# Attention into a gated convolution on one core: batch 0's x in rows of 4 KB, one maximum per batch on the read path, a new order of emission

## The chip, the cores and the metric

The kernel runs on one core of a Trainium2 chip. The metric is the device time of one execution in microseconds (us). The time before is 356.75 us, the median of 3 runs (355.89 to 357.86).

## The reference

Eight batches of attention in both directions between a sequence `x` (8 heads, 512 tokens, 64 wide) and a state of 32 tokens per head; the two results, put behind each other, are the 544 tokens of a gated feed-forward layer with a convolution over three tokens.

```
scores = scale * np.matmul(x, state.transpose(0, 1, 3, 2))
a = np.exp(scores - scores.max(-1, keepdims=True))
a /= a.sum(-1, keepdims=True) + 1e-09
xread = np.matmul(a, state)
scores2 = scale * np.matmul(state, x.transpose(0, 1, 3, 2))
a2 = np.exp(scores2 - scores2.max(-1, keepdims=True))
a2 /= a2.sum(-1, keepdims=True) + 1e-09
sread = np.matmul(a2, x)
t = np.concatenate([xread, sread], axis=2)         # heads side by side: 8 x 544 x 512
h = np.maximum(t @ w_in, 0.0)                       # 8 x 544 x 1024
conv_out[:, s] = sum of conv_w[k] * h[:, s + k - 1] for k in 0, 1, 2
out = (h / (1 + np.exp(-conv_out))) @ w_out         # 8 x 544 x 512
```

## The kernel before, in words

**Work.** The 1024 hidden columns are cut into 8 blocks of 128. A step is one block of one batch, 64 steps in all, named by a number `i` from 0 to 63 (batch `i // 8`, block `i % 8`): the hidden product into a bank `ps_h_i` (`hidden`, L630, six products of 512 columns), its rectified copy `h_i` (L200 on ScalarE, L202 on VectorE), the three taps into `t_i` (L194 or L196, then L673 and L678), the tanh (L682), the gate (L687), the split of the gated tile into two halves of fewer bits, `g0_i` (L205, ScalarE) and `g1_i` (L208, VectorE), and for each of four chunks `c` of 128 tokens three products into the bank `acc_b_c` (L705). A float32 product is made of three products of such halves (`PASSES`). After a batch's eighth block the chunks are copied out of their banks (L719 on ScalarE, L721 on VectorE) and stored (L740).

**The state's own tokens** go four batches at a time (`m` is 0 or 1), block by block, through the same layer: `ss_m_f` (L745, L749 twice, L752, L756), then `gts0_m_f` and `gts1_m_f` (L205, L208), then three products into `acc_t_m` (L705) and a store of four parts (L775). There is one buffer `ss`, so a block's chain begins when the last one's has ended.

**The read path** of a batch (what a state token reads of `x`): the scores' copy `at` is 128 rows by two head groups of 512; per group a maximum (`top`, L340), an exponential with its sum (`exp2`, L346), the reciprocal of that sum (`norm2`, L349 and L350), a transposition (`flip`, L355) and its copy, then `read` (L368) and a copy with the reciprocal as scale (`divide`, L375).

**Batch 0** has a path of its own, since nothing stands ahead of it. Its `x` comes as two tiles, each with all four pairs of heads and one half of the sequence, and everything is done by halves `q` of the sequence: `first_scores` (L320), the scaled copy of the scores (`keep_scores`, L194 or L196), `first_flip` (L488), the maximum (`first_top`, L492), the subtraction of it by TensorE (`first_shift`, L498), the exponential (L508), the sums (L512), their reciprocal (L516, L517), its spreading (L498), the division (L523), and the first hidden products (`first_hidden`, L637). The columns of the weights that batch 0 needs come as 64-bit words in tiles `raw_j` and are converted by ScalarE and VectorE on the way (L243 to L260), between the pieces of batch 0.

**Order.** Every operation of the program is entered in a list with what it reads and writes. Nothing schedules them: the table `ORDER`, written by hand, is a row of numbers of operations, and the program is emitted in that order; each engine does its part of it in that order. A `v` behind a number puts the operation on VectorE in place of ScalarE, and a negative number is so many products of zeros (L215) that keep TensorE occupied. SP issues the loads and all the stores but the last two, which ScalarE's own queue issues (`LAST`).

Of the kernel before, what the change touches and what calls it, by code (L numbers as in the profile page):

```python
# [953 lines left out]
```

## Time and profile before

| what | value |
|---|---|
| median of 3 runs | 356.75 us (355.89 to 357.86) |
| profiled execution | span 354.1 us; no other time of it is listed, and what lies around the span is taken as 356.75 - 354.1 = 2.65 us |
| TensorE (PE) busy | 98% of the span, 2538 products |
| VectorE (DVE) busy | 89% |
| ScalarE (ACT) busy | 72% |
| DMA | 35.06 MB, mean 99 GB/s |

The profile is one execution's trace. Its first line counts each engine's busy time; its chain of waits goes back from the last instruction to what released each; the groups of instructions give a mean time for one line, engine and shape; the timeline tells runs of like instructions in order with what ended the idle time before them; the windows give each engine's busy time, the granted clock and what the DMA engines moved in a stretch. The clock that TensorE was granted was 1.00 of full speed (2.4 GHz) in every stretch.

### The profile page before, as it was taken

Reading aid. Unit: us, or ns where it says so; the run is one execution under the profiler, and the core shown is the slowest. Engines: PE = TensorE matmul, PEld = TensorE weight load, DVE = VectorE, ACT = ScalarE, POOL = GpSimd, SP = SyncE. Lnnn points to the kernel's source line nnn. Section 1 sums busy time; section 2 is a strip of 40 time slices with the busy share of each in tenths; the row PEclk is TensorE's granted clock in tenths of the full one; section 3 lists DMA queues with packets and bytes.
Section 4 is the critical chain, followed back from the end, with each engine's and each line's share of the span. In section 5 each row is a group of like instructions: output and inputs, shape, how many; then the busy total and the mean of one; then the engine's idle time right before and its main releaser. Section 6 shows DMA issues by size and latency. Waiting matters only on the chain.

```text
span 354.1 us, 6694 instructions
## 1 busy us (share of the span) xinstructions
PE 348.6 (98%) x2538; PEld 271.8 (77%) x2538; DVE 316.1 (89%) x563; ACT 256.1 (72%) x560; POOL 29.4 (8%) x90
## 2 busy tenths in 40 slices
PE   7999999999999999999999999999999999999995
PEld 6766758876788868878789887878788868888884
DVE  1999999999999999999999999987799898889950
ACT  3999999998777997859856657774745447548642
POOL 1000000010000000100000300042201001113000
PEclk9999999999999999999999999999999999999999
DMA  7989998201600033030400000001200011000205
GB/s 255 396 309 377 328 357 302 62 1 50 219 0 2 0 127 142 3 119 32 180 30 2 0 31 31 30 3 60 89 2 0 0 71 65 2 2 0 74 33 176
DMA packets 13584, 35.06 MB, mean 99 GB/s; under 512 B 1520, under 2 KB 4720, under 8 KB 12528
## 3 DMA queue, kind: packets, MB, share of 16 engines
q1 hardware_dynamic: 12976, 34.28, 27.1%
q8 instruction: 20, 0.33, 0.4%
q10 hardware_dynamic: 576, 0.35, 0.3%
q14 instruction: 12, 0.10, 0.1%
HBM read 25.71 MB, written 8.91 MB: 98 GB/s over the span
## 4 chain that ended last, share of the span: by engine, by line
PE 97%; DMA 2%; ACT 0%; SPq 0%; issue 0%
PE acc L705 47%; PE ps_h L630 22%; PE ps_h L637 4%; PE ps_hs L615 4%; PE ps_u L548 4%; PE acc_t L705 3%; PE ps_r L368 2%; PE ps_t L355 2%; PE ps_s L310 2%; DMA xt<-xT 2%; PE acc_c L705 2%; PE acc L713 2%; PE ps_u L567 1%; PE ps_s L498 1%; PE ps_x L498 1%; PE ps_x L512 1%
## 5 line engine op out<-in xcount | busy, mean ns | idle before, releaser
L705 PE MATMUL acc<-wo,g 128*128 128x512 f32 x726 | 177.0, 393 | 0.0
L705 PEld LDWEIGHTS acc<-wo,g 128*128 128x128 f32 x726 | 134.7, 188 | 32.8 <-issue 1.7
L630 PE MATMUL ps_h<-a,u 128*128 128x512 f32 x336 | 83.2, 391 | 0.0
L630 PEld LDWEIGHTS ps_h<-a,u 128*128 128x128 f32 x336 | 62.7, 188 | 13.1
L682 ACT ACTIVATE t<-t 128x512 f32<-128x512 f32 x64 | 39.9, 630 | 14.5 <-DVE t L678 14.3
L673 DVE SCALAR_TENSOR_TENSOR t<-h,cw,t 128x511 f32<-128x511 f32 x64 | 47.1, 742 | 1.6 <-ACT t L194 1.5
L678 DVE SCALAR_TENSOR_TENSOR t<-h,cw,t 128x512 f32<-128x512 f32 (+1 forms) x64 | 46.8, 745 | 0.6
L205 ACT ACTIVATE g<-t 128x512 fp32r<-128x512 f32 (+1 forms) x62 | 37.5, 615 | 11.0 <-DVE t L687 5.5
L687 DVE SCALAR_TENSOR_TENSOR t<-t,h 128x512 f32<-128x512 f32 (+1 forms) x64 | 42.4, 667 | 2.3 <-ACT t L682 2.2
L208 DVE TENSOR_TENSOR g<-t,g 128x512 fp32r<-128x512 f32 (+1 forms) x62 | 41.3, 671 | 3.5 <-ACT g L205 3.1
L194 ACT ACTIVATE t<-h,cw 128x512 f32<-128x512 f32 x52 | 36.9, 723 | 4.3 <-DVE h L202 3.0
L200 ACT ACTIVATE h<-ps_h 128x512 f32<-128x512 f32 x56 | 33.3, 596 | 9.3 <-PE ps_h L630 6.1
L648 POOL COPY h<-hs 128x1 f32<-128x1 f32 x40 | 14.2, 376 | 129.2 <-ACT sr L383 66.3
L205 ACT ACTIVATE u<-ps_u 128x512 fp32r<-128x512 f32 x28 | 16.2, 596 | 8.5 <-PE ps_u L548 8.5
L719 ACT ACTIVATE o<-acc 128x512 f32<-128x512 f32 (+1 forms) x30 | 15.8, 544 | 8.5 <-PE acc L705 8.3
L648 POOL COPY hs<-h 128x1 f32<-128x1 f32 x40 | 13.6, 361 | 97.6 <-ACT h L200 80.9
L208 DVE TENSOR_TENSOR u<-ps_u,u 128x512 fp32r<-128x512 f32 x28 | 18.6, 682 | 2.5 <-ACT u L205 2.5
L615 PEld LDWEIGHTS ps_hs<-sr,wi 128*128 128x128 f32 x128 | 14.8, 192 | 1.1 <-ACT t L194 0.8
L637 PE MATMUL ps_h<-p,u 128*128 128x256 f32 x64 | 15.3, 386 | 0.0
L615 PE MATMUL ps_hs<-sr,wi 128*128 128x128 f32 x128 | 15.0, 276 | 0.0
L548 PE MATMUL ps_u<-wi,st 64*32 64x512 f32 x224 | 14.3, 597 | 0.0
L637 PEld LDWEIGHTS ps_h<-p,u 128*128 128x128 f32 x64 | 11.6, 190 | 3.3 <-DVE hc L249 0.8
(99 smaller groups left out, 400.3 us busy)
## 6 DMA issues: line engine op xcount, KB each, us to landing
xt<-xT SPq DMA_DIRECT2D x16, 512.0 KB, 7.7
xx<-xn SPq DMA_DIRECT2D x8, 1024.0 KB, 5.9
out<-o SPq DMA_DIRECT2D x27, 256.0 KB, 2.1
raw<-w_in SPq DMA_DIRECT2D x8, 512.0 KB, 7.6
raw<-w_out SPq DMA_DIRECT2D x8, 512.0 KB, 7.4
out<-o SPq DMA_DIRECT2D x6, 128.0 KB, 1.8
out<-o_t SPq DMA_DIRECT2D x8, 64.0 KB, 1.7
st<-stT SPq DMA_DIRECT2D x1, 448.0 KB, 10.2
```

What stands on the lines that cost most here:

```text
L194: A.activation(dst, src, AF.Copy, scale=scale)
L200: A.activation(dst, src, AF.Relu, scale=0.5)
L205: A.activation(hi, src, AF.Copy)
L208: engine.tensor_tensor(lo, src, hi.bitcast(F32), op=ALU.subtract)
L615: PE.matmul(ps_hs[m, f][:, :NT], wi[:, k, f * P:(f + 1) * P], sr[m][:, k, :], start=(k == 0), stop=(k == NK - 1))
L630: PE.matmul(ps_h[i], u[j][:, g, fs], a[k][:, g, :], start=(n == 0), stop=(n == 3 * NG - 1))
L637: PE.matmul(ps_h[f][:, q * HS:(q + 1) * HS], us[0, f // 4][0][:, g, f % 4 * P:(f % 4 + 1) * P], half_of(pa[0], q)[:, g, :], start=(g == 0) ...
L673: V.scalar_tensor_tensor(t[:, 1:], h[:, :S - 1], cw[:, f, 0:1], t[:, 1:], op0=ALU.mult, op1=ALU.add)
L678: V.scalar_tensor_tensor(t[:, :n], h[:, 1:n + 1], cw[:, f, 2:3], t[:, :n], op0=ALU.mult, op1=ALU.add)
L682: A.activation(tt[i], tt[i], AF.Tanh, scale=0.25)
L687: V.scalar_tensor_tensor(tt[i][:, :n], tt[i][:, :n], 1.0, hd[i][:, :n], op0=ALU.add, op1=ALU.mult)
L705: PE.matmul(acc, g[j][:, cs], wo[:, k, f, :], start=(f == 0 and n == 0), stop=(f == NF - 1 and n == 2))
```

## The change

Three things change. Batch 0's two tiles of `x` hold two pairs of heads and the whole sequence each (a row of 4 KB for each of 128 partitions, in place of four rows of 1 KB), as all other batches' do; each half of the first scores then reads both tiles. The read path's maximum is taken for both head groups of a batch by one operation over 128 x 1024, and the sum and its reciprocal are one operation each for both groups, so that both exponentials wait for the one maximum and the reciprocal for both exponentials. The table of the order is written anew: it has 35 operations on VectorE by `v` in place of 25, and the same 16 products of zeros (12 of them ahead of the first scores in place of 9).

```
     def xt_load(i):
         b, g = divmod(i, NG)
-        if b == 0:
-            xts[i] = buf([P, NP, HS], F32, "xt", f"xt_{i}")
-            nc.sync.dma_start(xts[i], xT[b, :, :, g * HS:(g + 1) * HS])
-            return
         xts[i] = buf([P, 2, S], F32, "xt", f"xt_{i}")
         nc.sync.dma_start(xts[i], xT[b, :, 2 * g:2 * g + 2, :])
...
-                PE.matmul(ps_s[q][g][j * NS:(j + 1) * NS, :HS], st[half, j, :], xts[q][half, j, :],
+                PE.matmul(ps_s[q][g][j * NS:(j + 1) * NS, :HS], st[half, j, :], half_of(xts[j // 2], q)[half, j % 2, :],
...
-    def top(i):
-
-        b, g = divmod(i, NG)
-        nm2[i] = buf([P, 1], F32, "nm2", f"nm2_{i}")
-        V.tensor_reduce(nm2[i], at[b][:, g, :], axis=AX.X, op=ALU.max, negate=True)
+    def top(b):
+        nm2[b] = buf([P, NG], F32, "nm2", f"nm2_{b}")
+        s2[b] = buf([P, NG], F32, "s2", f"s2_{b}")
+        V.tensor_reduce(nm2[b], at[b], axis=AX.X, op=ALU.max, negate=True)
...
-        s2[i] = buf([P, 1], F32, "s2", f"s2_{i}")
-        A.activation(e2[i], at[b][:, g, :], AF.Exp, bias=nm2.pop(i), accum_out=s2[i])
-
-    def norm2(i):
-        V.tensor_scalar_add(s2[i], s2[i], EPS)
-        V.reciprocal(s2[i], s2[i])
+        A.activation(e2[i], at[b][:, g, :], AF.Exp, bias=nm2[b][:, g:g + 1], accum_out=s2[b][:, g:g + 1])
+
+    def norm2(b):
+        V.tensor_scalar_add(s2[b], s2[b], EPS)
+        V.reciprocal(s2[b], s2[b])
...
-            add("PE", "scoresh", partial(first_scores, q), r=[("st", 0), ("xt", q)],
+            add("PE", "scoresh", partial(first_scores, q), r=[("st", 0)] + [("xt", g) for g in range(NG)],
...
-        A.activation(rr[b][:, g, :], ps_r[b][:, g * D:(g + 1) * D], AF.Copy, scale=s2.pop(i))
+        A.activation(rr[b][:, g, :], ps_r[b][:, g * D:(g + 1) * D], AF.Copy, scale=s2[b][:, g:g + 1])
...
-0 98 99 100 101 102 103 120 -9 123 121 125 -3 124 -1 142 143 126 2 -2 150 3 127 5 20 4 144 151 128 6 -1 152 132 145
+120 -3 0 -8 98 99 -1 101 100 102 103 121 123 124 2 126v 125 127 -1 140 141 4 148 149 3 5 142 14 15 17 150 128 16 129
```

Lines of the changed kernel lie four to six below those of the one before: the first scores stand in L316 (L320 before), the maximum in L335 (L340), the sum in L343 and L344 (L349, L350), the last copies in L715 and L717 (L719, L721).

**VectorE at the start of the program.** `hc` and `raw` are the weights under conversion, `heads` a small constant, `m0_q` the maxima of half `q` of batch 0, `nm2` the maximum of the read path, `ps_s_0_1_g` the second half's scores of head group `g`. A wait on a DMAHW semaphore is one for a landing. Before:

```order
L182 TENSOR_REDUCE heads_75<-ident_69 128x4 [waits Pool_49]
L492 TENSOR_REDUCE m0_0_146<-ps_x_0_141 128x16 [waits PE_49]
L340 TENSOR_REDUCE nm2_0_161<-at_0_112 128x1 [waits Activation_49]
L249 TENSOR_SCALAR hc_0_159<-hc_0_159 128x512 [waits Activation_49]
L492 TENSOR_REDUCE m0_1_183<-ps_x_1_154 128x16 [waits PE_49]
L252 ISA hc_0_159<-raw_0_150,hc_0_159 128x1024 [waits DMAHW4_49,DVE_49,Activation_49]
L340 TENSOR_REDUCE nm2_1_206<-at_0_112 128x1
L260 SCALAR_TENSOR_TENSOR wi_79<-raw_0_150,hc_0_159 128x4x128 [waits DVE_49]
```

With the change:

```order
L196 TENSOR_SCALAR at_0_117<-ps_s_0_1_0_128 128x256 [waits PE_49]
L196 TENSOR_SCALAR at_0_117<-ps_s_0_1_1_129 128x256 [waits PE_49]
L182 TENSOR_REDUCE heads_75<-ident_69 128x4 [waits Pool_49]
L335 TENSOR_REDUCE nm2_0_144<-at_0_117 128x2 [waits DVE_49,Activation_49]
L488 TENSOR_REDUCE m0_0_153<-ps_x_0_148 128x16 [waits PE_49]
L488 TENSOR_REDUCE m0_1_161<-ps_x_1_156 128x16 [waits PE_49]
L249 TENSOR_SCALAR hc_0_163<-hc_0_163 128x512 [waits Activation_49]
L249 TENSOR_SCALAR hc_2_184<-hc_2_184 128x512 [waits Activation_49]
L252 ISA hc_0_163<-raw_0_138,hc_0_163 128x1024 [waits DMAHW4_49,DVE_49]
L252 ISA hc_2_184<-raw_2_182,hc_2_184 128x1024 [waits DMAHW5_49,DVE_49,Activation_49]
L260 SCALAR_TENSOR_TENSOR wi_79<-raw_0_138,hc_0_163 128x4x128 [waits DVE_49]
L260 SCALAR_TENSOR_TENSOR wi_79<-raw_2_182,hc_2_184 128x2x256 [waits DVE_49]
```

The copies of the second half's scores come onto VectorE, and the one wide maximum stands ahead of both of the halves' maxima; before, a maximum of the read path stood behind each of them.

**TensorE at the start.** `idle` are products of zeros, `ps_x_q` the transposed scores. Of the eight first scores of each half those that wait are shown, and of other groups the first. Before:

```order
L215 MATMUL idle_102<-zeros_67 128x128 x8
L320 MATMUL ps_s_0_0_0_113<-xt_0_100,st_81 32x256 [waits DMAHW1_49,DMAHW0_49]
...
L215 MATMUL idle_102<-zeros_67 128x128 x3
L320 MATMUL ps_s_0_1_0_130<-xt_1_123,st_81 32x256 [waits DMAHW3_49]
...
L215 MATMUL idle_102<-zeros_67 128x128
L488 MATMUL ps_x_0_141<-ident_69,at_0_112 128x128 [waits Activation_49,Pool_49]
...
L215 MATMUL idle_102<-zeros_67 128x128 x2
L488 MATMUL ps_x_1_154<-ident_69,at_0_112 128x128 [waits Activation_49]
...
L498 MATMUL ps_s_0_0_0_113<-eight_74,m0_0_146 32x128 [waits DVE_49,Pool_49]
...
L215 MATMUL idle_102<-zeros_67 128x128
L498 MATMUL ps_s_0_1_0_130<-eight_74,m0_1_183 32x128 [waits DVE_49]
```

With the change:

```order
L215 MATMUL idle_93<-zeros_67 128x128 x11
L316 MATMUL ps_s_0_0_0_118<-xt_0_91,st_81 32x256 [waits DMAHW1_49,DMAHW0_49]
...
L316 MATMUL ps_s_0_0_0_118<-xt_1_115,st_81 32x256 [waits DMAHW3_49]
...
L316 MATMUL ps_s_0_1_0_128<-xt_0_91,st_81 32x256
...
L215 MATMUL idle_93<-zeros_67 128x128
L484 MATMUL ps_x_0_148<-ident_69,at_0_117 128x128 [waits Activation_49,Pool_49]
...
L484 MATMUL ps_x_1_156<-ident_69,at_0_117 128x128 [waits DVE_49]
...
L494 MATMUL ps_s_0_0_0_118<-eight_74,m0_0_153 32x128 [waits DVE_49,Pool_49]
...
L494 MATMUL ps_s_0_1_0_128<-eight_74,m0_1_161 32x128 [waits DVE_49]
```

The first half's scores wait for both landings and not for one; the second half's follow at once, and the transpositions and shifts of the two halves stand together.

**The end of the program.** On TensorE, each row shown is followed by one with `g0` (or `gts0`) in place of `g1` (or `gts1`), two products, which is left out without a mark. Before:

```order
L705 MATMUL acc_t_1_3619<-wo_80,gts1_1_7_3928 128x512
L705 MATMUL acc_7_1_3789<-wo_80,g1_61_3889 128x512
L705 MATMUL acc_7_2_3761<-wo_80,g1_62_3908 128x512
L705 MATMUL acc_7_3_3737<-wo_80,g1_62_3908 128x512
L705 MATMUL acc_7_0_3741<-wo_80,g1_61_3889 128x512
L705 MATMUL acc_7_1_3789<-wo_80,g1_62_3908 128x512
L705 MATMUL acc_7_1_3789<-wo_80,g1_63_3935 128x512
L705 MATMUL acc_7_3_3737<-wo_80,g1_63_3935 128x512
L705 MATMUL acc_7_2_3761<-wo_80,g1_63_3935 128x512
L705 MATMUL acc_7_0_3741<-wo_80,g1_62_3908 128x512
L705 MATMUL acc_7_0_3741<-wo_80,g1_63_3935 128x512
```

With the change:

```order
L701 MATMUL acc_7_1_3736<-wo_80,g1_62_3829 128x512
L701 MATMUL acc_7_1_3736<-wo_80,g1_63_3864 128x512
L701 MATMUL acc_7_3_3756<-wo_80,g1_63_3864 128x512
L701 MATMUL acc_7_2_3681<-wo_80,g1_62_3829 128x512
L701 MATMUL acc_7_2_3681<-wo_80,g1_63_3864 128x512
L701 MATMUL acc_7_0_3695<-wo_80,g1_60_3790 128x512
L701 MATMUL acc_t_1_3573<-wo_80,gts1_1_6_3880 128x512
L701 MATMUL acc_t_1_3573<-wo_80,gts1_1_7_3929 128x512
L701 MATMUL acc_7_0_3695<-wo_80,g1_61_3807 128x512
L701 MATMUL acc_7_0_3695<-wo_80,g1_62_3829 128x512
L701 MATMUL acc_7_0_3695<-wo_80,g1_63_3864 128x512
```

The first use of `g1_63` moves from 15 products ahead of the end to 30, that of the last block of the state's tokens (`gts1_1_7`) from 33 to 12, and that of the block ahead of it (`gts1_1_6`, in an earlier row before) from 51 to 15. The last hidden product of step 63, ahead of these rows, moves from 165 products before the end to 105. On VectorE, the same stretch before:

```order
L749 SCALAR_TENSOR_TENSOR ss_1_7_3879<-hs_83,cw_78,ss_1_7_3879 128x128 [waits Activation_49]
L208 TENSOR_TENSOR g1_61_3889<-t_61_3662,g0_61_3888 128x512 [waits Activation_49]
L749 SCALAR_TENSOR_TENSOR ss_1_7_3879<-hs_83,cw_78,ss_1_7_3879 128x128 [waits DVE_49]
L687 SCALAR_TENSOR_TENSOR t_63_3724<-t_63_3724,h_63_3708 128x512
L687 SCALAR_TENSOR_TENSOR t_62_3753<-t_62_3753,h_62_3652 128x512
L721 TENSOR_SCALAR o_6_2_0_3910<-acc_6_2_3417 128x512 [waits DMAHW4_49,DMAHW7_49,DMAHW3_49,DMAHW0_49]
L756 SCALAR_TENSOR_TENSOR ss_1_7_3879<-ss_1_7_3879,hs_83 128x128 [waits Activation_49]
L208 TENSOR_TENSOR g1_62_3908<-t_62_3753,g0_62_3907 128x512 [waits Activation_49]
L208 TENSOR_TENSOR gts1_1_7_3928<-ss_1_7_3879,gts0_1_7_3927 128x128 [waits Activation_49]
L208 TENSOR_TENSOR g1_63_3935<-t_63_3724,g0_63_3934 128x512 [waits Activation_49]
L721 TENSOR_SCALAR o_7_1_0_3972<-acc_7_1_3789 128x256 [waits Activation_49]
```

With the change:

```order
L674 SCALAR_TENSOR_TENSOR t_63_3754<-h_63_3725,cw_78,t_63_3754 128x512
L683 SCALAR_TENSOR_TENSOR t_63_3754<-t_63_3754,h_63_3725 128x512 [waits Activation_49]
L208 TENSOR_TENSOR g1_63_3864<-t_63_3754,g0_63_3863 128x512 [waits Activation_49]
L745 SCALAR_TENSOR_TENSOR ss_1_6_3873<-hs_83,cw_78,ss_1_6_3873 128x128 [waits Activation_49]
L745 SCALAR_TENSOR_TENSOR ss_1_6_3873<-hs_83,cw_78,ss_1_6_3873 128x128 [waits DVE_49]
L752 SCALAR_TENSOR_TENSOR ss_1_6_3873<-ss_1_6_3873,hs_83 128x128 [waits Activation_49]
L208 TENSOR_TENSOR gts1_1_6_3880<-ss_1_6_3873,gts0_1_6_3879 128x128 [waits Activation_49]
...
L745 SCALAR_TENSOR_TENSOR ss_1_7_3900<-hs_83,cw_78,ss_1_7_3900 128x128 [waits Activation_49]
L745 SCALAR_TENSOR_TENSOR ss_1_7_3900<-hs_83,cw_78,ss_1_7_3900 128x128 [waits DVE_49]
L752 SCALAR_TENSOR_TENSOR ss_1_7_3900<-ss_1_7_3900,hs_83 128x128 [waits Activation_49]
...
L208 TENSOR_TENSOR gts1_1_7_3929<-ss_1_7_3900,gts0_1_7_3928 128x128 [waits Activation_49]
```

The chain of step 63 (`t_63`, `g1_63`) comes ahead of the last two blocks of the state's tokens, which now stand one behind the other at the very end.

## Rows read from the trace of the kernel before

**Rows 1.** The page: busy time, and the chain that ended last, by engine
```profile
PE 348.6 (98%) x2538; PEld 271.8 (77%) x2538; DVE 316.1 (89%) x563; ACT 256.1 (72%) x560; POOL 29.4 (8%) x90
...
PE 97%; DMA 2%; ACT 0%; SPq 0%; issue 0%
```

**Rows 2.** Groups by form: busy us, mean ns | idle before, for products of L705
```profile
L705 PE MATMUL acc<-wo,g 128*128 128x512 f32 x726 | 177.0, 393 | 0.0
```

**Rows 3.** Timeline of PE at 299 us: start, us, line, count
```profile
299.12 3.79 PE L705 MATMUL acc<-wo,g 128*128 128x512 f32 x16
```

**Rows 4.** Timeline of the first 20 us: start, us, engine, line, [idle, releaser]
```profile
0.71 1.31 SPq L295 DMA_DIRECT2D xt<-xT  x2
...
5.07 0.67 PE L320 MATMUL ps_s<-xt,st 64*32 64x256 f32 x16 [0.33 <-DMA xt<-xT]
...
6.53 0.43 SPq L894 DMA_DIRECT2D st<-stT  x1
...
7.17 0.67 PE L320 MATMUL ps_s<-xt,st 64*32 64x256 f32 x16 [0.57 <-DMA xt<-xT]
...
8.73 0.69 DVE L492 TENSOR_REDUCE m<-ps_x 128x16 f32<-128x512 f32 x1 [2.85 <-PE ps_x L488]
...
9.57 1.08 PE L498 MATMUL ps_s<-eight,m 128*32 128x128 f32 x32
...
11.00 1.08 PE L498 MATMUL ps_s<-eight,m 128*32 128x128 f32 x32
...
18.07 1.99 PE L637 MATMUL ps_h<-p,u 128*128 128x256 f32 x8
```

**Rows 5.** Windows at the start: PE, PEld, DVE, ACT, POOL, clock, DMA share, GB/s
```profile
4.00:6.00 2.00, 1.67 (x25) 1.09 (x25) 0.74 (x4) 0.53 (x3) 0.00 (x0) 1.00 1.03 323
...
6.00:8.00 2.00, 1.43 (x24) 0.83 (x23) 0.00 (x0) 0.55 (x3) 0.00 (x0) 1.00 1.06 381
...
14.00:16.00 2.00, 2.00 (x42) 1.80 (x39) 2.00 (x4) 2.00 (x6) 0.00 (x0) 1.00 1.02 406
```

**Rows 6.** Groups by form of the VectorE operations removed, added and moved
```profile
L340 DVE TENSOR_REDUCE nm<-at 128x1 f32<-128x512 f32 x16 | 10.8, 679 | 0.0
...
L437 DVE TENSOR_REDUCE m<-af 128x32 f32<-128x1024 f32 x7 | 8.5, 1215 | 0.1
...
L350 DVE RECIPROCAL s<-s 128x1 f32<-128x1 f32 x16 | 2.6, 164 | 0.5
...
L349 DVE TENSOR_SCALAR s<-s 128x1 f32<-128x1 f32 x16 | 2.3, 144 | 0.0
...
L721 DVE TENSOR_SCALAR o<-acc 128x256 f32<-128x256 f32 x1 | 0.4, 424 | 6.2 <-ACT o L719 6.2
```

**Rows 7.** Windows behind the start, columns as in rows 5
```profile
18.07:28.85 10.78, 10.78 (x148) 7.35 (x144) 10.72 (x22) 10.51 (x23) 0.00 (x0) 1.00 0.92 327
28.85:49.72 20.87, 20.83 (x254) 13.52 (x248) 20.35 (x44) 20.20 (x51) 0.00 (x0) 1.00 0.96 349
```

**Rows 8.** Timeline of the end
```profile
338.36 1.29 DVE L687 SCALAR_TENSOR_TENSOR t<-t,h 128x512 f32<-128x512 f32 x2
...
341.40 0.69 DVE L208 TENSOR_TENSOR g<-t,g 128x512 fp32r<-128x512 f32 x1 [0.15 <-ACT g L205]
...
343.57 6.96 PE L705 MATMUL acc<-wo,g 128*128 128x512 f32 x30
...
350.57 0.66 ACT L719 ACTIVATE o<-acc 128x256 f32<-128x256 f32 x2 [0.70 <-PE acc L705]
```

**Rows 9.** Groups by form of the chains of step 63 and of the state's tokens
```profile
L682 ACT ACTIVATE t<-t 128x512 f32<-128x512 f32 x64 | 39.9, 630 | 14.5 <-DVE t L678 14.3
...
L687 DVE SCALAR_TENSOR_TENSOR t<-t,h 128x512 f32<-128x512 f32 x56 | 37.9, 683 | 2.3 <-ACT t L682 2.2
...
L749 DVE SCALAR_TENSOR_TENSOR ss<-hs,cw,ss 128x128 f32<-128x128 f32 x32 | 11.0, 345 | 1.1 <-ACT ss L745 0.9
...
L752 ACT ACTIVATE ss<-ss 128x128 f32<-128x128 f32 x16 | 4.9, 304 | 7.4 <-DVE ss L749 7.2
```

More of the change, by code (lines that the diff above doesn't have):

```diff
@@ L119 @@
[L119 to L120 removed]
+120 -3 0 -8 98 99 -1 101 100 102 103 121 123 124 2 126v 125 127 -1 140 141 4 148 149 3 5 142 14 15 17 150 128 16 129
+-1 6 143 131 151 20 8 18 144 7 21 9 22 19 23 11 145 -1 24 10 26 27 133 134 12 152 153 25 13 50 196 445 446 146 147 154
+52 447 155 51 451 132 29 28 448 450 30 32 33 34 35 473 53 54 449 452 36 -1 31 37 453 1 185 186 188 195 198 199 200 201
@@ new lines @@
+1032 1033 1046 397 398 1009 992 1007 1060 1022 1024 1034 352 1057 1058 1023 1035 1038 353 1047 1074 354 1507 399 400
+1088 1039 1519 1006 1021 1515 1036 1037 355 1520 1521 1522 1523 356 361 1108 1089 1090 1075 1524 1061 1525 1526 1153
+1062 1109 1110 1048 1049 1063 1064 1050 1154v 1156 1155 1138 1054 1065 1076 1077 1139 974 975 1142v 1078 1141 1140
+1052 1067 1527 1079 1528 1529 1143 1144 1530 1145 1087 1091 1053 1532 1051 1066 1073 1080 1533 1123 1124 1092 1093 394
+362 365 1534 1146 1535 1536 1068 1083 973 366 1094 363 1081 1069 1084 1095 364 1112v 1113 395 1531 1096 1100 1101 1147
@@ new lines @@
+1082 1127v 1128 1183 1184 1198 1098 1187 1185 1186 1126 1114 1115 1168 1116 1117 1104 1125 1129 1130 1236 1118 1122
+1199 1131 1188 1105 1200 1132 1133 1111 1537 1538 1169 1172v 1099 1540 1157v 1119 1158 1159 1106 1107 1148 1170 1541
+1097 1542 1202v 1203 1102v 1204 1213 1160 1171 1137 1134 1543 1205 1149 1214v 1215 1161 1201 1544 1173 1174 1545 1546
+1237v 1239 1103 1120 1135 1150 1152 1121 1136 1251 1162 1266 1163 1164 1175 1176 1189 1151 1166 1217 1548 1252 401
+1218 1190 1191 1206 1165 433 1177 1178 1181 1240 1180 1192 1193 1539 1167 1182 1267 1269 1219 1220 1221 1238 1241 1222
@@ new lines @@
+1223 1207 1208 1281 1196 1211 1549 1226 1195 1550 1551 1179 1194 1209 402 403 1282v 404 1255 1256 1283 405 1242 1243
+1244 1270 1271 1224 1253 1257 1552 1197 1212 1258 1268 1272 1285v 1286 1228 1273 1259 1326 1274 1229 1327 1553 1227
+1341 1330v 1328 1342 1343 1554 1216 1331 1556 1557 1558 1559 1210 1225 1230v 1231 1275 1276 1245 1234v 1296 1246 1311
+1312 1287 1254 1344 1315v 1313 435 436 438 1329 437 1260 1261 1560 1297 1300v 440 1250 1332 1547 1555 443 1248 1298
+1263 1265 1278 1247 439 1299 1288 1289 434 1316 1317 1561 1562 441 1284 444 1301 1302 442 1314 1379 1569 1570 1380
@@ new lines @@
+1381 1235 1345 1563 1564 1232v 1382 1303 1566 1567 1233 1304 1262 1249 1277 1364 1264 1279 1439 1394 1318 1319 1346
+1347 1290 1280 1291 1293 1365 1367 1366 1305 1306 1333 1320 1308 1321 1571 1323 1334 1368 1369 1348 1440 1442 1443v
+1294 1309 1572 1573 1383 1574 1575 1565 1384 1444 1385 1292 1307 1585 1386 1387 1295 1310 1324 1335 1336 1395v 1576
+1339 1325 1349 1454 1586 1397 1587 1588 1441 1445 1589 1590 1591 1338 1446 1447 1350 1340 1409 1351 1568 1322 1337
+1577 1578 1396 1579 1580 1353 1352 1398 1399 1424 1354 1455 1410 1411 1370 1371 1388 1372 1389 1581 1400 1582 1583
@@ L121 @@
+1373 1360 1361 1425 1457 1374 1377 1413v 1593 1594 1414 1401 1458 1415 1375 1402 1403 1392 1355 1412 1459 1595 1596
+1597 1584 1416 1469 1470v 1598 1417 1356 1357 1599 1404 1376 1391 1418 1419 1592 1456 1472 1609 1473v 1378 1393 1390
[3 rows of a table added]
+1498v 1499 1625 1626 1467 1496 1627 1628 1629 1497 1489 1482 1494 1495 1490v 1491 1435 1624 1630 1631 1632 1450 1492v
+1633 1635 1637 1636 1465 1493 1480 1486 1484 1634 1485 1487
 """
@@ L388, in attention @@
             i = NG * b + g
-            add("SP", "load_xt" if b else "load_xth", partial(xt_load, i), w=[("xt", i)])
+            add("SP", "load_xt", partial(xt_load, i), w=[("xt", i)])
         add("SP", "load_x2", partial(x_load, b), w=[("xx", b)])
@@ L400, in attention @@
                 w=[("scores", b, g)] + [("at", b)] * (b > 0 and g == 0))
+        rows_of = [("at", b)] + [("scores", b, q) for q in range(NG)]
+        add("DVE", "wide", partial(top, b), r=rows_of, w=[("nm2b", b), ("s2b", b)])
         for g in range(NG):
             i = NG * b + g
-            rows_of = [("at", b)] + [("scores", b, q) for q in ([g] if b else range(NG))]
-            add("DVE", "red", partial(top, i), r=rows_of, w=[("nm2", i)])
-            add("ACT", "exp2", partial(exp2, i), r=rows_of + [("nm2", i)], w=[("e2", i), ("s2", i)])
-            add("DVE", "norm2", partial(norm2, i), w=[("s2", i)])
+            add("ACT", "exp2", partial(exp2, i), r=rows_of + [("nm2b", b), ("s2b", b)], w=[("e2", i), ("s2", i)])
+        add("DVE", "norm2", partial(norm2, b), r=[("s2", NG * b + g) for g in range(NG)], w=[("s2b", b)])
+        for g in range(NG):
+            i = NG * b + g
             add("PE", "flip", partial(flip, i), r=[("e2", i)], w=[("ps", "t", i)])
@@ L411, in attention @@
         for g, i in enumerate(pair):
-            add("ACT", "rr", partial(divide, i), r=[("ps", "r", b), ("s2", i)] + [("rr", b)] * g,
+            add("ACT", "rr", partial(divide, i), r=[("ps", "r", b), ("s2b", b)] + [("rr", b)] * g,
                 w=[("rq", b, g)] if g else [("rq", b, g), ("rr", b)])
```

32 lines of the change are left out of this document (10 added, 22 removed), and 64 rows, old and new, of the table ORDER.

## The prediction

> **What bounds the kernel now.** I read the page's busy line and chain first: TensorE is busy 348.6 of 354.1 us and the chain that ended last lies on it for 97% [rows 1]. So an operation of VectorE or ScalarE counts only where TensorE waits for it. Next, how full TensorE's own time is: the mean of a 512-column product is 393 ns [rows 2], but products overlap, and sixteen in a row take 3.79 us, of which the last is one whole mean, so the pitch is (3.79 - 0.39) / 15 = 0.227 us [rows 3]. The change removes no product of the real work, and the products of zeros stay 16. That leaves the two ends of the program. At the start [rows 4] TensorE waits for batch 0's x twice, at 5.07 and 7.17 us, and for VectorE's first maximum until 9.57, and the first hidden products stand at 18.07. At the end, 30 products from 343.57 and then a copy and a store are all that is left [rows 8]. In between, the windows show PE busy for the whole stretch, and VectorE nearly as full: 10.72 of 10.78 us and 20.35 of 20.87 us [rows 7]. A saving on VectorE could show there, if anywhere.
>
> The sum is made against the profiled span of 354.1 us. The median of the runs, 356.75, lies 2.65 above it, and I add that at the end. A difference under 0.5% (1.78 us) is about what a measurement of this kernel can't tell from no change.
>
> **Loads of batch 0's x.** Before, the first half's scores start at 5.07 behind the first load, the second half's at 7.17 behind the second [rows 4]. With the change both halves need both loads. No row shows these two tiles in long rows, so I bound the time X of the second landing: not before the first landing of before (scores at 5.07), and not later than the second (7.17). For an earlier landing speaks that the DMA moved 323 GB/s (4 to 6 us) and 381 (6 to 8) while short rows were in flight, and 406 GB/s later (14 to 16), at the same busy share [rows 5]; and the issue of such a load took SP 1.31 / 2 = 0.65 us, that of one with one row per partition 0.43 [rows 4], so the second load is issued some 0.2 us sooner. One megabyte at 406 in place of 323 to 381 GB/s saves 0.2 to 0.7 us. I take X = 6.1, the middle of the bounds, a little more than those two savings give.
>
> The Trainium skill ("DMA: Bandwidth & Descriptors", section Specifications) gives 512 B as the least transfer for line rate; by that, rows of 1 KB have nothing to gain. The windows [rows 5] lean against it, though other work shared them. By the rule X would stay near 7.17; that is rival 3 below, which is worked out from rows.
>
> **From X to the first hidden product.** Scores of both halves run one behind the other, 2 x 0.67 less overlap, to X + 1.25. ScalarE copies the first half, VectorE now the second: two copies of 256 columns at 0.42 [rows 6] to X + 2.1. Then VectorE does the small constant (0.3, an estimate from the copies' 0.42 for twice its columns), the wide maximum at about 1.2 (the like reduction over 128 x 1024 took 1.215 [rows 6]) and only then the first half's maximum (0.69 [rows 4]). The first shift so starts at about X + 4.2, the second a maximum later, and ends at X + 4.2 + 0.7 + 1.08 + a hand-over = X + 6.2. Before, the second shift ended at 11.00 + 1.08 = 12.08, and the hidden product came 6.0 later, at 18.07 [rows 4]. What stands between (exponentials, sums, spreading, division, the first weights) is the same, in another order; with 6.2 for it, the hidden product comes at X + 12.4 = 18.5, 0.4 later than before. Here the wide maximum costs: what waits behind it is both halves' maxima, and TensorE waits for those. It pays back on VectorE: two maxima at 0.679 become one of about 1.215, and one pair of 0.144 + 0.164 goes [rows 6], 0.14 + 0.31 = 0.45 us per batch. As VectorE is full behind 18.07 [rows 7], I count 0.3 of batch 0's as regained. **Start: +0.1** (X = 5.07: -0.9; X = 7.17: +1.2).
>
> **Maxima and sums of the other batches.** 7 x 0.45 = 3.2 us less on VectorE, all of it hidden beside products. The bound downwards is half of the first four batches' 1.8, about -1.0, for the stretches where VectorE is full [rows 7]; the bound upwards is the wait that is added: a batch's second exponential waits no longer for its own maximum alone, at most one maximum of 0.54 later (1.215 - 0.679), and behind it lie whole hidden products of the batch before. Ten operations more go to VectorE by the table, at 0.4 to 0.7 each, which eats the saving up. **0.**
>
> **Loads behind the first two.** SP's later loads stand in another order, and the wait of one holds the next; all of them are needed microseconds behind the stretch in which they are issued. **0**, its cover being the running weights' conversion; if it goes, that is in the range.
>
> **The end.** Counted in the order, 150 products lay between step 63's last hidden product and the first use of `g1_63`; now 75 do, 75 x 0.227 = 17.0 us. VectorE has 26 operations in that span: sixteen of 512 columns at about 0.70 [rows 8, 9], nine on the state's tokens at about 0.31 [rows 9], one near 0.5, 14.5 us by their durations. Neighbours overlap (two of 0.683 in 1.29 [rows 8, 9], 0.08 for each pair), so 12.7 back to back. Waits for ScalarE on the way: two of a full tile (0.63 and a hand-over of 0.2 each), two of a side tile (0.30 and 0.2 each), 1.0 for the rest: 3.6. With 0.4 to begin, `g1_63` is ready 16.7 us behind the product, 0.3 ahead of its use. Before, it was done at 342.09 [rows 8], and its use was the sixteenth product of the 30 behind 343.57, at about 346.97: 4.9 us ahead. Then come the last two blocks of the state's tokens through the one buffer `ss`: a chain of two taps (0.345), a tanh (0.304), a gate, a split, with hand-overs about 3.5 us for the last of them, ready at 21.8 to 21.9; it is used 18 products behind the first use of `g1_63`, 17.0 + 4.1 = 21.1. That leaves a wait of 0.2 to 0.8, of which I count 0.2, as the chain's first copy and taps can slide beside the copies of the output. The closing copy and store [rows 8] are unchanged, so there is nothing to gain. **End: +0.2** (0 to +2.0).
>
> **Sum**: 354.1 + 0.1 + 0 + 0.2 = 354.4, with 2.65 around it **357.0 us**.
>
> **The rivals.**
>
> *1. Faster: x lands by 5.1 and VectorE's saving passes on.* Then the start gives -0.9 and the relief -1.0: 354.85. For it: VectorE's windows are full right where TensorE's work is made of small pieces [rows 7]. Against it: PE's own busy time there is whole too, so there is little idle time to close, and the wide maximum sits on the critical chain.
>
> *2. Slower: the chain at the end becomes the bound.* The place is VectorE between the last hidden product and `g1_63` and `gts1_1_7`. It decides as soon as VectorE is later than 17.0 us behind that product, against my 16.7; each microsecond beyond passes to the end in full, as only 30 products are left. Priced from [rows 9]: if each of the 26 operations costs its full duration with no overlap, 1.8 us more, the wait is 1.5 us, and the chain of `ss` adds 0.5: +2.0, with the start 358.85. Against it: the neighbours that the trace shows do overlap [rows 8], and the two waits for ScalarE that I price at most may fall together with work in front of them.
>
> *3. The load doesn't do what it says: the pair of tiles lands at 7.17.* Then waiting for both costs what the first half gained from coming early: +1.2 + 0.2, 358.15.
>
> **Numbers.** My forecast (no change that shows) 0.53, rival 1 0.17, rival 2 0.16, rival 3 0.14. The range runs from 354.4 (a little below rival 1) to 358.9 (rival 2), which leaves out under 2 in 10. Faster by over 0.5% (below 354.97) takes rival 1 and a little of my own case's lower side: 0.20. Slower (above 358.53) takes most of rival 2 and a part of rival 3: 0.18. The rest, 0.62, is the same.
>
> **What would show it.** Timeline of the start: first scores at 6.1 (5.1 for rival 1, 7.2 for rival 3), the first shift 4.2 later, the first hidden product near 18.5. Windows: PE busy throughout from there. Groups: one reduction over 128 x 1024 to 128 x 2 at about 1.2 us, eight times. End: `g1_63` done within a microsecond of its use, and PE's idle time ended by VectorE's `gts` near the end, under a microsecond. Wrong would be: PE waiting in the middle for a load or for a maximum, or a hidden product of batch 0 over 1 us from 18.5.

## The result, and the profile after

| | before | changed |
|---|---|---|
| median of 13 runs each | 356.75 us | 359.07 us |
| ratio, 95% interval | | 1.0051 [1.0035, 1.0068] |
| the ratio in us on 356.75 | | 358.6 [358.0, 359.2] |
| span of the profiled execution | 354.1 us | 356.4 us |

The change made the kernel about half a per cent slower, at the border of what counts here as no change. (The two medians lie 0.65% apart; the ratio is not that of the medians, and I go by it.) The profiled execution of the changed kernel took 358.19 us, 0.9 below its median and 1.8 above its span. With the same 1.8 around it, that of before took 355.9, also 0.9 below its median: the two traces may be set against each other, and differ by 2.3 us. Of the 2.65 us that the sum of the prediction puts around the span, 1.8 are so what lies around it, and 0.9 the distance of that trace from the median.

The page of the changed kernel, busy line and chain (answering [rows 1]):

```profile
PE 348.0 (98%) x2538; PEld 272.9 (77%) x2538; DVE 321.1 (90%) x550; ACT 251.8 (71%) x549; POOL 31.6 (9%) x90
...
PE 81%; DVE 10%; DMA 4%; ACT 3%; SPq 1%; issue 1%; DVEq 0%; ACTq 0%
```

TensorE does the same products and is busy for as long, but the chain that ended last now runs over VectorE for a tenth and over DMA for 4%. TensorE's waits, by engine and line: us in total, times, longest.

```profile
PE ps_s L494 <- DVE m L488: 1.6, 1, 1.6
PE ps_u L544 <- DMA st<-stT: 1.1, 1, 1.1
...
PE ps_s L316 <- DMA xt<-xT: 0.6, 1, 0.6
PE ps_s L306 <- DMA xt<-xT: 0.2, 1, 0.2
PE acc_t L701 <- DVE gts L208: 0.2, 1, 0.2
```

Two are in the start (L494 and L316), two are new ones on a landing (L544 on the second part of the states, L306 on an x tile), one is at the end. Timeline of the start, beside [rows 4]:

```profile
0.71 0.88 SPq L294 DMA_DIRECT2D xt<-xT  x2
...
5.51 0.64 PE L316 MATMUL ps_s<-xt,st 64*32 64x256 f32 x8
...
6.78 1.07 PE L316 MATMUL ps_s<-xt,st 64*32 64x256 f32 x24 [0.63 <-DMA xt<-xT]
...
8.76 1.22 DVE L335 TENSOR_REDUCE nm<-at 128x2 f32<-128x1024 f32 x1
...
9.90 1.28 DVE L488 TENSOR_REDUCE m<-ps_x 128x16 f32<-128x512 f32 x2
...
10.72 1.95 PE L494 MATMUL ps_s<-eight,m 128*32 128x128 f32 x64 [1.58 <-DVE m L488]
...
18.88 1.13 PE L633 MATMUL ps_h<-p,u 128*128 128x256 f32 x4
```

The scores of both halves run from 6.78, VectorE takes the wide maximum and then both halves' maxima, and the first hidden product comes at 18.88, 0.8 later than before. Then SP's issues, and TensorE:

```profile
8.87 0.43 SPq L294 DMA_DIRECT2D xt<-xT  x1
14.32 0.33 SPq L239 DMA_DIRECT2D raw<-w_in  x1
14.69 1.32 SPq L890 DMA_DIRECT2D st<-stT  x1
```

```profile
19.85 0.38 PE L215 MATMUL idle<-zeros 128*128 128x128 f32 x2
21.35 1.09 PE L544 MATMUL ps_u<-wi,st 64*32 64x512 f32 x16 [1.12 <-DMA st<-stT]
22.68 1.09 PE L306 MATMUL ps_s<-xt,st 64*32 64x512 f32 x16 [0.24 <-DMA xt<-xT]
```

SP issues nothing between 8.87 and 14.32 us: the load that stands there needs a buffer that the conversion of an earlier piece still holds, and behind it stand the states of batches 1 to 7 (L890), issued at 14.69 and landed at 21.2. TensorE waits for them, and then for an x tile.

Windows behind the start, in the stretches of [rows 7], columns as there:

```profile
18.07:28.85 10.78, 9.42 (x98) 6.53 (x95) 9.22 (x17) 8.84 (x20) 0.00 (x0) 1.00 0.98 367
28.85:49.72 20.87, 20.82 (x310) 14.31 (x309) 20.55 (x40) 20.87 (x53) 0.00 (x0) 1.00 0.85 312
```

VectorE's 10.72 of 10.78 us became 9.22, ScalarE's 10.51 became 8.84: the engines that were full before stood idle for 1.6 and 1.9 us. Groups by form (answering [rows 6]):

```profile
L335 DVE TENSOR_REDUCE nm<-at 128x2 f32<-128x1024 f32 x8 | 9.7, 1213 | 1.3 <-ACT at L194 1.3
...
L344 DVE RECIPROCAL s<-s 128x2 f32<-128x2 f32 x8 | 1.3, 166 | 0.3
...
L343 DVE TENSOR_SCALAR s<-s 128x2 f32<-128x2 f32 x8 | 1.3, 157 | 0.0
```

and the end (answering [rows 8]):

```profile
344.58 0.69 DVE L208 TENSOR_TENSOR g<-t,g 128x512 fp32r<-128x512 f32 x1 [0.76 <-ACT g L205]
...
349.58 0.29 DVE L208 TENSOR_TENSOR gts<-ss,gts 128x128 fp32r<-128x128 f32 x1
...
349.92 0.96 PE L701 MATMUL acc_t<-wo,gts 128*128 128x512 f32 x3 [0.20 <-DVE gts L208]
...
350.72 2.21 PE L701 MATMUL acc<-wo,g 128*128 128x512 f32 x9
...
352.97 0.66 ACT L715 ACTIVATE o<-acc 128x256 f32<-128x256 f32 x2 [1.45 <-PE acc L701]
```

TensorE's last nine products are held by the last tile of the state's tokens, ready at 349.87.

To see where time goes when the order differs, I laid each trace's products end to end at the least pitch of their kind (0.227 us for 512 columns, products of zeros at nothing) and took how late a trace is with its work at a given time. It is an account of one execution, and the pitch taken for the small products moves the gap between the two rows at 20 and 45 us by some 0.4; the gaps at 343 us and at the last product do not hang on it:

| us behind that pitch at | 20 us | 28 us | 45 us | 343 us | last product |
|---|---|---|---|---|---|
| before | 8.6 | 8.7 | 9.5 | 12.0 | 11.8 |
| changed | 9.0 | 10.8 | 11.1 | 13.8 | 14.2 |

So 0.4 us were lost by 20 us and 2.1 by 28, half a microsecond of it came back by 45, 0.2 went between there and 343, and 0.6 in the end.

### The profile page after: what moved, and what is told of

The parts are those of the page before. It is cut to its first block, busy times and chain, and to the rows that moved or that the text cites. A ratio compares the mean times of both kernels' runs of the same rounds, so it can differ in the third digit from the quotient of the medians.

```text
span 356.4 us, 6672 instructions
## 1 busy us (share of the span) xinstructions
PE 348.0 (98%) x2538; PEld 272.9 (77%) x2538; DVE 321.1 (90%) x550; ACT 251.8 (71%) x549; POOL 31.6 (9%) x90
## 4 chain that ended last, share of the span: by engine, by line
PE 81%; DVE 10%; DMA 4%; ACT 3%; SPq 1%; issue 1%; DVEq 0%; ACTq 0%
PE acc L701 39%; PE ps_h L626 20%; PE ps_h L633 4%; PE ps_hs L611 4%; PE ps_u L544 3%; PE ps_r L362 2%; PE acc_t L701 2%; DMA raw<-w_in 2%; PE ps_t L349 2%; PE ps_s L306 2%; DMA xt<-xT 2%; DVE g L208 2%; PE acc_c L701 2%; PE acc L709 1%; DVE t L683 1%; DVE t L674 1%
## 5 line engine op out<-in xcount | busy, mean ns | idle before, releaser
L194 ACT ACTIVATE t<-h,cw 128x512 f32<-128x512 f32 x45 | 32.1, 720 | 0.4 <-DVE g L208 0.3
L644 POOL COPY hs<-h 128x1 f32<-128x1 f32 x40 | 16.5, 424 | 111.6 <-ACT h L200 72.8
L644 POOL COPY h<-hs 128x1 f32<-128x1 f32 x40 | 15.0, 391 | 116.1 <-DVE t L683 93.0
L715 ACT ACTIVATE o<-acc 128x512 f32<-128x512 f32 (+1 forms) x27 | 14.7, 552 | 8.9 <-PE acc L701 8.8
L544 PE MATMUL ps_u<-wi,st 64*32 64x512 f32 x224 | 14.3, 597 | 1.1 <-DMA st<-stT 1.1
L243 ACT ACTIVATE hc<-raw 128x512 f32<-128x512 f32 (+1 forms) x17 | 10.9, 664 | 4.5 <-DMA raw<-conv_w 4.0
```

The source lines that it names most:

```text
L194: A.activation(dst, src, AF.Copy, scale=scale)
L644: G.tensor_copy(dst, src)
```

## The experiments

All ratios are to the kernel before, run on the same chip beside them; pieces of `ORDER` are shown with "..." where it goes on.

**Are the new waits on loads the loss?** The first kernel moves two issues on SP:

```
-... 50 196 445 446 ... 453 1 185 186 188 195 198 ...
+... 50 196 1 195 445 446 ... 453 185 186 188 198 ...
```

> The changed kernel, with SP's issue of the states of batches 1 to 7 and of x tile 4 moved ahead of the load of weight piece 5, which waits 5.4 us for a buffer. Loads theory (SP's queue lost most of the time: TensorE waits 1.1 us for the states and 0.2 for x tile 4 behind 20 us): both waits shrink to under 0.2 us and the span falls from 356.4 to 354.8 to 355.3. Rival (the operations: the wide maximum ahead of both halves' maxima, and VectorE's added copies): the span stays at 356.1 to 356.7, as the wait turns up at the next operation of VectorE.

Measured: 358.37 us, ratio 1.0041 [1.0026, 1.0055], span 356.1. The wait for the states is gone, the time hardly moved; in its trace TensorE stands 0.49 us for ScalarE at 22.5 us instead. The second moves the early load of w_out's first block (operation 50) and its conversion (51 to 54) back, which also frees the buffer SP waited for:

```
-... 25 13 50 196 ... 154 52 447 155 51 451 ... 473 53 54 449 ... 43 156 501 ... 161 55 162 ...
+... 25 13 196 ... 154 447 155 451 ... 473 449 ... 43 156 50 501 ... 161 51 52 53 54 55 162 ...
```

> The changed kernel, with the load and the conversion of the first block of w_out moved behind the loads that the first two batches need. Loads theory: that early load of 512 KB and the buffer it takes (for which the load of weight piece 5 waits) are the cause, so the states land before 19 us, both waits of TensorE go, and the span is 354.6 to 355.2. Rival (a plain wait for the weights that VectorE and ScalarE convert): the states land earlier, but the hidden products wait for the converted pieces instead, and the span stays above 356.

Measured: 358.29 us, ratio 1.0038 [1.0023, 1.0054], span 356.4. TensorE's waits in that trace, and its timeline where the new one ends:

```profile
PE ps_s L495 <- DVE m L489: 1.6, 1, 1.6
PE acc L710 <- DVE t L684: 1.2, 1, 1.2
```

```profile
43.81 3.77 PE L710 MATMUL acc<-whole,t 128*128 128x512 f32 x8 [1.19 <-DVE t L684]
```

Both waits on loads are gone and at 28 us the trace is 9.1 us behind, 0.4 more than before. But by 45 it is 11.1 behind, exactly as the changed kernel: TensorE stands 1.2 us for VectorE at the first products of gated tiles. The loads theory is wrong as a cause of the span, which it put at 354.6 to 355.2: behind the wait that was seen stood another, of VectorE and ScalarE, that ends at the same time. In the changed kernel the first of these products starts at 43.98. In the kernel before it starts at 41.31, with one group of sixteen scores (1.0 us) less ahead of it.

I then shifted two of VectorE's operations out of the places where it stood idle in that trace:

```
-... 200 201 38 ... 189 499 ... 161 51 52 53 54 55 162 205 492 207 ...
+... 200 38 ... 189 201 499 ... 161 51 52 162 205 492 53 54 55 207 ...
```

> The kernel of e2_wout_later, with two places of VectorE's order changed: batch 2's wide maximum two operations later (VectorE stood 0.74 us for it at 23 us), and the late w_out block's conversion behind batch 1's maximum (0.86 us at 33). Theory (up to the first product of gated tiles, near 44 us, VectorE and ScalarE are the bound, and each microsecond in which VectorE stands idle there is a microsecond of the span): that product starts at 42.0 to 42.7 in place of 43.8 and the span is 354.7 to 355.4. Rival (that product waits for the amount of work, not for the gaps): it stays at 43.6 to 43.9 and the span at 356.2 to 356.5.

Measured: 358.07 us, ratio 1.0040 [1.0025, 1.0056], span 357.2; the product in question starts at 43.97. The theory failed in this form: VectorE's idle time only moved (1.28 us at 24 us, waiting for ScalarE). What holds 44 us was not found by moving single operations.

**Which part of the change costs what, in the old order?** The table of before, applied to the new operations (the second x tile issued ahead of the first scores, each wide operation at the place of the first of its two where both halves are there):

> The order of the kernel before (with its products of zeros) for the operations of the changed kernel: the pair loads and the wide maxima and sums stand, the issue of the second x tile moved ahead of the first scores, each wide operation at the place of the first of its two where both halves are there. Theory (the order lost the time, the operations cost nothing): a span of 353.8 to 354.6 and a time within 0.3% of the kernel before. Rival (the operations lost it): a span of 355.5 or more.

Measured: 359.04 us, ratio 1.0060 [1.0040, 1.0079], span 357.8. The rival: in the old order the operations lose as much as the whole change. Split up, the loads alone in the kernel before (with the change's `xt_load` and `first_scores`):

```
-... 120 -9 123 121 125 ...
+... 120 -9 121 123 125 ...
```

> The kernel before in its own order, with the pair loads of batch 0's x alone (the second load issued ahead of the first scores). Theory (the first half's scores lose their head start of 1.7 us, and VectorE and ScalarE, the bound up to 44 us, stand idle for it): 0.7 to 1.5 us slower, span 354.8 to 355.6. Rival (what the prediction took: the pair lands earlier and most is regained): span 353.8 to 354.5.

Measured: 357.66 us, ratio 1.0028 [1.0006, 1.0049], span 355.6. The ratio is less sure than it looks: one of the twelve executions, 360.67 us at a granted clock of 0.95, lifts it, and the median is 0.13% above that of the runs beside it. Its timeline of TensorE:

```profile
6.79 0.64 PE L317 MATMUL ps_s<-xt,st 64*32 64x256 f32 x8 [0.25 <-DMA xt<-xT]
...
7.35 0.94 PE L216 MATMUL idle<-zeros 128*128 128x128 f32 x6
...
8.21 0.66 PE L317 MATMUL ps_s<-xt,st 64*32 64x256 f32 x16
...
10.61 1.08 PE L495 MATMUL ps_s<-eight,m 128*32 128x128 f32 x32
```

The pair landed for 6.79, but the second half's scores started at 8.21, behind the products of zeros that the old order has between the halves. And the wide maxima and sums alone, with the loads of before:

```
-        nm2[i] = buf([P, 1], F32, "nm2", f"nm2_{i}")
-        V.tensor_reduce(nm2[i], at[b][:, g, :], axis=AX.X, op=ALU.max, negate=True)
...
+        V.tensor_reduce(nm2[b], at[b], axis=AX.X, op=ALU.max, negate=True)
```

(and the sum and the reciprocal likewise)

> The kernel before in its own order and with its own loads, with the wide maxima and sums alone, each at the place of the first of its two where both halves' scores are there. Theory (an exponential now waits for both groups' scores and the longer maximum, and in an order made for two maxima ScalarE stands for it): 1 to 2.5 us slower, span 355.1 to 356.6. Rival (hidden, or VectorE's relief passes on): span 353.0 to 354.3.

Measured: 358.10 us, ratio 1.0033 [1.0017, 1.0050], span 356.1. Here the wait for both groups is seen, on ScalarE and then on VectorE:

```profile
30.03 0.72 ACT L345 ACTIVATE e<-at,nm 128x512 f32<-128x512 f32 x1 [1.58 <-DVE nm L340]
...
32.58 0.17 DVE L348 TENSOR_SCALAR s<-s 128x2 f32<-128x2 f32 x1 [0.87 <-ACT e L345]
```

On TensorE two waits are seen that the kernel before doesn't have:

```profile
PE ps_s L499 <- DVE m L493: 0.5, 1, 0.5
PE ps_t L354 <- ACT e L345: 0.4, 1, 0.4
```

The second (at 30.90 us) stands behind that exponential. The first (at 11.62) is of another kind: batch 0's wide maximum stands on VectorE ahead of the second half's maximum, for which the second shift waits. How the cost divides between the two was not tried.

The sums without the maxima, in the kernel before:

```
-        A.activation(e2[i], at[b][:, g, :], AF.Exp, bias=nm2.pop(i), accum_out=s2[i])
...
+        A.activation(e2[i], at[b][:, g, :], AF.Exp, bias=nm2.pop(i), accum_out=s2[b][:, g:g + 1])
...
-        V.tensor_scalar_add(s2[i], s2[i], EPS)
-        V.reciprocal(s2[i], s2[i])
...
+        if summed[b] == NG:
+            V.tensor_scalar_add(s2[b], s2[b], EPS)
+            V.reciprocal(s2[b], s2[b])
```

> The kernel before with the merged sums and reciprocals alone (one pair of operations per batch; loads, maxima and order as before). Theory (what the wide operations cost in the old order, 2.0 us, is the maximum's wait for both head groups; the sums only relieve VectorE): span 353.6 to 354.3. Rival (the sums' wait for both exponentials, 0.87 us in the trace of e9_before_wide, costs too): span 354.6 to 355.4.

Measured: 357.05 us, ratio 0.9997 [0.9985, 1.0010]. No difference: the sums neither cost nor give, so that by difference the wide maximum carries the cost (it was not run without the merged sums). (Its profiled span, 355.3 at a time equal to its median, shows how far one trace's span may lie from another's without any difference in the medians.) In the old order, 0.28% for the loads and 0.33% for the wide operations make 0.61%, and both together measured 0.60%. That agreement is not to be leaned on: each interval reaches about 0.2 either way, and by the medians it is 0.13% and 0.25% against 0.63%.

**Do the parts cost anything in the new order?** Undoing the wide operations in place:

```
-        V.tensor_reduce(nm2[b], at[b], axis=AX.X, op=ALU.max, negate=True)
+        for g in range(NG):
+            V.tensor_reduce(nm2[b][:, g:g + 1], at[b][:, g, :], axis=AX.X, op=ALU.max, negate=True)
```

(and the sum and the reciprocal likewise)

> The changed kernel, with the maximum and the sum of the read path again one operation for each head group, in the same places of the order. Theory (the saving of 0.45 us of VectorE per batch is hidden beside products): the span is 356.4 to 356.9, the first shift 0.1 to 0.2 us later. Rival (VectorE's relief passes on to TensorE where VectorE is full): 1 to 2 us slower, 357.4 to 358.4.

Measured: 359.77 us, ratio 1.0073 [1.0046, 1.0101], span 357.0, between the theory's and the rival's. Undoing the loads:

```
+        if b == 0:
+            xts[i] = buf([P, NP, HS], F32, "xt", f"xt_{i}")
+            nc.sync.dma_start(xts[i], xT[b, :, :, g * HS:(g + 1) * HS])
+            return
...
-                PE.matmul(ps_s[q][g][j * NS:(j + 1) * NS, :HS], st[half, j, :], half_of(xts[j // 2], q)[half, j % 2, :],
+                PE.matmul(ps_s[q][g][j * NS:(j + 1) * NS, :HS], st[half, j, :], xts[q][half, j, :],
```

> The changed kernel with batch 0's x loaded by halves of the sequence again (rows of 1 KB), everything else and the order as changed. Theory (the pair loads give up the first half's head start; the new order, which runs both halves together, has no use for it any more): the first half's scores at 5.1, the second half's at 7.1 in place of 6.8, the first shift 0.3 later, span 356.4 to 356.8. Rival (the head start still helps, as in the old order, where the pair loads cost 1.5 us): span 355.0 to 355.6.

Measured: 359.18 us, ratio 1.0064 [1.0042, 1.0087], span 358.3, outside both forecasts. Neither undoing gains; both point to slower than the change's 1.0051, but the intervals overlap, so that stays unresolved. In the second's trace the second half's scores came late, 1.7 us behind those of the kernel before, so that it is no clean return to the old loads:

```profile
8.84 0.67 PE L320 MATMUL ps_s<-xt,st 64*32 64x256 f32 x16 [2.54 <-DMA xt<-xT]
```

So the operations cost 0.6% in the old order, the whole change 0.51%, not told apart, and with one operation undone the new order still stands 0.64% or 0.73% above the kernel before. The new table of the order then gives back nothing that shows of what the operations cost, and it may well cost as much by itself; the new order with both operations undone was not run.

**The start's chain.** Batch 0's wide maximum behind both halves' maxima:

```
-... 126v 125 127 -1 140 141 4 148 149 3 ...
+... 126v 125 -1 140 141 4 148 149 127 3 ...
```

> The changed kernel with batch 0's wide maximum behind both halves' maxima on VectorE. Theory (VectorE's sum of work to 44 us is the bound, not the order of three of its operations): the first shift comes 1.1 us earlier, at 9.5 to 9.7, the first hidden product at 18.3 to 18.9, and the span stays at 356.1 to 356.5. Rival (the wait of TensorE for the first shift passes to the end): span 355.2 to 355.5.

Measured: 358.31 us, ratio 1.0051 [1.0033, 1.0069], the changed kernel's ratio. The first shift came at 9.53, 1.2 earlier, as expected, and no gain is seen. That isn't a clean answer: in its trace the first hidden product came at 22.29, where 18.3 to 18.9 was expected, and TensorE's clock fell in between (last section); eleven of its twelve executions were granted 0.995 or less on the mean, where all thirteen of the changed kernel had 0.999 or 1.00. The one that was granted 0.999 took 358.32 us, no less than the best of the changed kernel (358.09).

**The end.** The chain of the state's tokens' block 6 in the gaps of step 63's gate:

```
-... 1475 1608 1476 1477 1478 1479 1616 1468 1617 1618 1619 1620 1621 1622 1623 1451 ...
+... 1475 1608 1617 1618 1619 1476 1620 1477 1478 1621 1479 1622 1623 1616 1468 1451 ...
```

> The changed kernel, with the chain of the state's tokens of block 6 laid into the gaps of step 63's gate, so that block 7's chain starts some 1.9 us earlier. Theory (the wait of 0.36 us of acc_t's last products at 349.6 and the slower products beside it are what the end lost): the last product starts 0.4 to 0.6 us earlier and the span is 355.8 to 356.1. Rival (the row of stores on SP behind acc_t sets the end): the wait goes and the span stays at 356.3 to 356.5.

Measured: 357.80 us, ratio 1.0022 [1.0003, 1.0041], span 356.1, the best of the variants of the changed kernel. TensorE's wait for `gts` is no longer in its list, and the last product starts 0.25 us earlier, less than expected: block 7's chain began only 0.6 earlier, as ScalarE had a copy of the output ahead of it. The ratio points to more than the trace shows, at overlapping intervals.

**All together**, with batch 0's x by halves, the first half ahead of the second, w_out late, and this end:

```
-... 121 123 124 2 126v 125 127 -1 140 141 4 148 149 3 5 142 14 15 17 150 ... 143 ...
+... 121 123 2 125 140 124 141 126v 142 4 127 148 3 5 143 149 -1 14 15 17 150 ...
```

> The changed operations with half loads, the first half's transposition, maximum, shift and exponential ahead of the second half's, w_out's first block late as in e2_wout_later, and the end of e7_tail. Theory (the start and the idle time of VectorE and ScalarE before 44 us hold the loss): first shift near 8.1, span 354.5 to 355.5, about as the kernel before. Rival (the first product of gated tiles stays at 43.7 whatever stands ahead): span 356.0 to 356.4.

Measured: 359.00 us, ratio 1.0061 [1.0037, 1.0085]. Worse than forecast: in its trace the second load landed at 9.27, the first shift came at 10.35 in place of 8.1, and the first product of gated tiles starts at 47.53; but that execution was the longest of the seven (361.31 us), and TensorE's clock fell in it. No version tried beats the kernel before.

## Why the prediction was right or wrong, point by point

The forecast was 357.0 (354.4 to 358.9) and no change that shows. Measured is 358.6 by the ratio, inside the range, and slower by 0.51% where 0.5% was the border: as the interval holds the border, it stays undecided whether that is the likeliest case, no change that shows, or just beyond it. The sum was 1.6 us too low, and between the two traces the loss is 2.3 us where the sum had 0.3. That the range held the time is partly luck: its upper end was made for a wait of 2 us at the end of the program, and by the account at least half of the loss lies ahead of 45 us.

**What bounds the kernel** was read too narrowly, and as far as the runs show this is the step that made the sum too low: that VectorE and ScalarE count only where TensorE is seen to wait for them. TensorE is busy for 98%, but that doesn't make it the bound at the start. Up to 44 us VectorE and ScalarE were full as well [rows 7], and three variants that took away quite different waits of TensorE (e1, e2, e6) all met again at 43.7 to 44.0. I used that row only for a saving that might pass on, not for a loss. That the two engines are the bound there is argued from this and not shown: the run made to show it (e6) failed.

**Loads of batch 0's x.** X was taken at 6.1 and measured 6.74 (scores from 6.78); the bounds held. The pair brought the second landing forward by 0.4 us (7.13 to 6.74), 0.25 of it because the load was issued sooner (1.18 us in place of 1.43). The two savings that I had read from the rows, 0.4 to 0.9 together, so held at their low end; what failed is the step beyond them to the middle of the bounds, for which no row spoke. Rival 3, the pair no earlier than 7.17, did not come. From 2 to 8 us the trace of before moved 1.89 MB (241, 323 and 381 GB/s) and that of the change 1.92 MB (202, 378 and 380); the four other traces with halves moved 1.71 to 1.83 MB, the eight others with pairs 1.89 to 1.96, with other loads beside them. The Trainium skill's rule ("DMA: Bandwidth & Descriptors", Specifications: line rate from 512 B) would leave long rows no gain; the first two traces agree with it nearly, the others lean against it, and no run separates row length from the rest.

**X to the first hidden product** was right: first shift 4.0 behind X (4.2 forecast), hidden product 12.1 behind it (12.4). With the later X it came at 18.88, 0.8 later than before, and 0.4 by the account of work at 20 us. That the 0.3 of VectorE's relief would be regained was wrong: at 45 us nothing of it is seen. And the whole term may matter less than its size: the shift 1.2 us earlier showed no gain in e11, though there the clock fell.

**Maxima and sums: 0** was right for the sums (0.9997, in the old order). For the maxima the reason that I gave doesn't hold in every order: I put the added wait at 0.54 us with whole hidden products behind it. In the old order, where the exponentials stand close behind, it costs 0.33% (e9), with 1.58 us on ScalarE at one place and 0.4 to 0.5 us twice on TensorE. In the changed kernel no such wait of ScalarE stands at an exponential (0.2 us in the whole trace, against 2.2 in e9's), and undoing the wide form gained nothing (e3), so no run shows the term wrong there.

**Loads behind the first two: 0** is the term that failed most plainly. I named the cover and left it at that; in the trace SP waits for a buffer in front of the states, 5.4 us between two issues. It cost TensorE 1.1 and 0.2 us, and half a microsecond came back by 45. It is also one of the signs of being wrong that the prediction names: PE waiting for a load. Yet this is not what made the time, since e1 and e2 took it away for 0.1%, which their intervals don't tell from nothing.

**The end: +0.2** was right in mechanism. `g1_63` was done at 345.27 and used at once (forecast 0.3 ahead); the last tile was ready at 349.87 and held TensorE 0.36 us beyond the pitch. By the account the end lost 0.6, three times the term but within its bounds. Rival 2 came in this small form: the chain at the end did become the bound, by tenths and not by 2 us.

**What stays open**: which operations of VectorE and ScalarE hold the first product of gated tiles at 44 us in the new order. Of the kernels with the new order that moved what stands ahead of it, none starts it sooner than 43.74 (e1). A start by itself settles little: e13's trace has it at 42.02, 0.7 later than the kernel before, with no difference in the time. So the cause of the loss stays open.

## What to carry to other kernels

Where three engines are full together, read the stretch's windows of all of them: a wait that one engine shows may have another behind it that ends at the same time, and removing the first then buys nothing. Merging two operations of which the first could start early trades time on the engine for a wait for both inputs; in an order that was fitted to the early start the wide maxima were paid for (e9), while merging the sums cost nothing (e13), so each merge is worth a run of its own. When loads are issued in order from one queue, look for a load that waits for a buffer and list what stands behind it.
